# Attention into experts: the first item's last x slots turned by VectorE at the end of attention instead of by TensorE inside the expert stage

## The chip, the cores and the metric

One core of one Trainium2 chip. The time is the device time of one execution in microseconds (us), median of three runs. Engines are named as in the profile: PE is TensorE (PEld its weight loads), DVE is VectorE, ACT is ScalarE, POOL is GpSimd, SP is the engine that issues nearly all DMAs.

## What is computed

Attention with random features, whose output is the input of a mixture of experts with one expert per token:

```python
# attention: q, k, v are (4, 8, 576, 64), omega (128, 64)
q_p, k_p = phi(q * scale), phi(k * scale)   # phi(x): exp(h - max(h)) / sqrt(128), h = x @ omega.T - |x|^2 / 2
kv = einsum('bhsm,bhsd->bhmd', k_p, v)
num, den = einsum('bhsm,bhmd->bhsd', q_p, kv), einsum('bhsm,bhm->bhs', q_p, k_p.sum(2)) + 1e-06
x = (num / den).transpose(0, 2, 1, 3).reshape(2304, 512)
# experts: 8, capacity 576 each; w1 (8, 512, 1024), w2 (8, 1024, 512)
expert = argmax(x @ w_gate, 1); gate = softmax at expert
out[i] = gate[i] * (relu(x[i] @ w1[expert]) @ w2[expert])   # for tokens within the capacity, else 0
```

## The kernel before, in words

**Attention.** The main loop runs over steps: 18 for the keys, then t = 0 to 20 for the 18 tiles of 128 queries. Step t projects tile t on TensorE (pjq), transposes tile t - 2 (qtr), and accumulates numerator, denominator and gate logits of tile t - 3 into qacc (`numer`, L634). ScalarE exponentiates the two qtr banks into qpT (L802). `normalise` (L644) on VectorE divides: den (L650), rec (L652), xr (L653), and lg, the sum of the gate logits over the heads (L659). xr is written to x_d in HBM (L660). qacc has a single buffer, two PSUM banks, so the accumulation of the next tile starts when xr of the last one has been read.

**Experts.** An item is up to 576 slots of one expert. Its two matrix products use three float32r passes each: both operands are split into an upper part (hi, rounded) and a lower part (lo, the remainder). `mm1` (L666) makes one hi group: 12 matmuls for 128 rows of the hidden layer, over slots 0 to 255 (half 0) or 256 to 575 (half 1), followed by hhii (ScalarE, upper part after relu, L682) and hlo (VectorE, lower part, L685); hi groups go round three PSUM banks. x is needed with its 512 columns on the partitions: xhi and xlo are 128 x 4 x 576.

**The first item** is started inside attention. Its expert is known from the first token in step 3. Its x is the first 576 rows of attention's output. Tiles 0 and 1 (slots 0 to 255) are transposed on TensorE straight from xr in steps 5 to 8 (`FIRST_AT`). In step 15 `first_rows` (L625) loads x_d rows 256 to 639 with one DMA. Steps 18 to 20, when there is nothing left to project, each take one hi group of half 0 (`AHEAD`). After the loop the first item's other groups follow; ahead of the first three of these `transpose_x` (L394) transposes slots 256 to 575 on TensorE, 128, 128 and 64 at a time, and `copy_x` copies them to xhi (ScalarE, L408) and xlo (VectorE, L410).

**Later items** get x in another way. `load_x` (L380) loads 576 rows with four DMAs, one for each quarter of the columns, in blocks of 32 rows, and `turn_x` (L386) lets VectorE transpose 32 x 32 squares (L388). A column 4p + k then lies on partition p, part k, so w1 is loaded by rows 4p + k, `"(p k)"`, instead of rows 128k + p, `"(k p)"`, which the TensorE way needs. `run` and `start` work small tasks off between the parts of a step; the order of instructions on each engine is the order in which the program writes them.

```python
if 0 <= t - 3 < NT:                      # L814, end of a step
    normalise(t - 3, acc_l[0])
...
if j == 0 and k < 3:                     # L933, first item, ahead of a hi group
    for _ in transpose_x(2 + k, nm, (SM, 3, None)[k]):
        pass
mm1(f, half, hhi, hlo, hf, nm)()
```

Of the kernel before, what the change touches and what calls it, by code (L numbers as in the profile page):

```python
# [22 lines left out]
NT = N // 128  # L23
# [33 lines left out]
def attention_moe(ctx, tc, kT, qT, va, om, wg, w1, w2, cap, ident, tri, desc, lst, tab0, out):  # L57
# [83 lines left out]
    def start(gen):  # L141
        tasks.append([gen, None])

    def run(at=None, times=1, most=99):
        for _ in range(times):
            for task in list(tasks):
                if task[1] is None or (task[1] == at and most > 0):
                    most -= task[1] is not None
                    try:
                        task[1] = next(task[0])  # L150
                    except StopIteration:
                        tasks.remove(task)
# [197 lines left out]

    def load_w(i, c, ev, chunks_of="(k p)"):
        if i == 1:
            src = w1[ds(ev, 1), :, c * 256 : (c + 1) * 256].rearrange(f"o {chunks_of} f -> p (o k) f", p=128)
        else:
            src = w2[ds(ev, 1), c * 256 : (c + 1) * 256, :].rearrange("o (k p) f -> p (o k) f", p=128)
        nc.sync.dma_start(w_raw[i][c], src)
# [18 lines left out]
                in_offset=bass.IndirectOffsetOnAxis(ap=big["idx"][0:n, i, 2:3], axis=0),  # L377
            )

    def load_x(row):  # L380
        src = x_d[ds(row, SLOTS), :].rearrange("(b r) (q c) -> q r b c", r=32, q=4)
        for q in range(4):
            nc.sync.dma_start(big["xz"][32 * q : 32 * q + 32, :, :], src[q])


    def turn_x(b0, b1):  # L386
        t = big["xt"][:, 0 : b1 - b0, :].rearrange("p b (k r) -> p b k r", k=4)
        nc.vector.transpose(t, big["xz"][:, b0:b1, :].rearrange("p b (a k) -> p b k a", k=4))  # L388
        t = t.rearrange("p b k r -> p k b r")
        hi, lo = (big[x][:, :, 32 * b0 : 32 * b1].rearrange("p k (b r) -> p k b r", r=32) for x in ("xhi", "xlo"))  # L390
        nc.scalar.copy(hi, t)
        nc.vector.tensor_tensor(lo, t, hi.bitcast(F32), op=ALU.subtract)

    def transpose_x(i, nm, at):  # L394
        n = sub_n[i]
        tr = pair(f"xtr{nm}{i}") if at is None else bank(at, f"xtr{nm}{i}")
        for k in range(4):
            nc.tensor.transpose(
                tr[:, k * n : (k + 1) * n], big["xg"][0:n, i, k * 128 : (k + 1) * 128], id_sb[0:n, 0:n]
            )  # L400
        yield from copy_x(tr, i * SUB, n)
# [221 lines left out]
    xr_l = {}  # L623

    def first_rows():  # L625
        nc.sync.dma_start(
            big["xg"][:, 2:, :], x_d[2 * SUB : NSUB * SUB, :].rearrange("(i p) d -> p i d", p=SUB)
        )

    def numer(t, qpT, acc):  # L630
        for p in range(NP):
# [11 lines left out]

    def normalise(t, acc):  # L644
        xr = small.tile([128, ROW, H], F32, tag="xr", name=f"xr{t}", bufs=4)
        if t < 2:
            xr_l[t] = xr
        av = acc.rearrange("p (i x) -> p i x", i=2)[:, :, 0 : NP * ROW].rearrange("p i (h c) -> p c i h", c=ROW)
        den = small.tile([128, H], F32, tag="den", name=f"den{t}")
        nc.vector.tensor_scalar(den.rearrange("p (i h) -> p i h", i=2), av[:, D, :, :], EPS, None, op0=ALU.add)  # L650
        rec = small.tile([128, H], F32, tag="rec", name=f"rec{t}")
        nc.vector.reciprocal(rec, den)  # L652
        nc.vector.tensor_tensor(  # L653
            xr.rearrange("p c (i h) -> p c i h", i=2),
            av,
            rec.rearrange("p (i h) -> p i h", i=2).unsqueeze(1).to_broadcast([128, ROW, 2, NP]),
            op=ALU.mult,
        )
        nc.vector.tensor_reduce(lg[:, t, :], xr[:, D + 1 : ROW, :], op=ALU.add, axis=AX.X)  # L659
        nc.sync.dma_start(x_d[t * 128 : (t + 1) * 128, :], xr[:, 0:D, :].rearrange("p c h -> p (c h)"))  # L660

    HALVES = [(0, 256), (256, SLOTS)]

# [40 lines left out]
    for n in range(NK + NT + 3):  # L704
# [20 lines left out]
        if 0 <= t - 2 < NT:  # L725
            d = d_l.pop(t - 2)
            trs = [bank(3 + i, f"qtr{n}{i}") for i in range(2)]

            parts = [
                [(trs[i][:, u * 64 : (u + 1) * 64], d[64 * i : 64 * i + 64, u, :], i) for u in range(H)] for i in range(2)  # L730
            ]

            if t in FIRST_AT:
                k0 = FIRST_AT.index(t)
                i = k0 % 2
                tr = bank(SM, f"xtri0{k0}")
                rows = slice(64 * i, 64 * i + 64)
                x0 = xr_l[k0 // 2][:, 0:D, :].rearrange("p c h -> p (c h)")
                parts[i][0:0] = [
                    (tr[:, k * 64 : (k + 1) * 64], x0[rows, k * 128 : (k + 1) * 128], i) for k in range(4)  # L740
                ]
                start(copy_x(tr, 64 * k0, 64))
            for x in chain(*zip_longest(*parts)):
                if x is not None:
                    rows = slice(64 * x[2], 64 * x[2] + 64)
                    nc.tensor.transpose(x[0], x[1], id_sb[rows, rows])  # L746
# [42 lines left out]
        else:  # L789
# [24 lines left out]
            if 0 <= t - 3 < NT:  # L814
                normalise(t - 3, acc_l[0])
                if t == 3:
                    start(first_item())
            run(times=3)
        if 0 <= t < NT and t - QB[c] == 2 and c + 2 < len(QB) - 1:
            load_q(c + 2)  # L820
# [78 lines left out]
    with ExitStack() as ifs:  # L899
        for j in range(B):  # L900
# [15 lines left out]
            def prefetch():  # L916
                nonlocal row
                if last:
                    return
                ev = nc.sync.value_load(resd[0:1, 0, j : j + 1], min_val=0, max_val=E - 1)  # L920
                row = nc.sync.value_load(resd[0:1, 1, j : j + 1], min_val=0, max_val=N - S)
                load_x(row)
                for c in range(4):
                    load_w(1, c, ev, "(p k)")
                yield
                for c in range(4):
                    load_w(2, c, ev)
                yield

            pre = prefetch()  # L930
            for k, (f, half) in enumerate(STEPS[j > 0]):

                if j == 0 and k < 3:  # L933
                    for _ in transpose_x(2 + k, nm, (SM, 3, None)[k]):
                        pass
                mm1(f, half, hhi, hlo, hf, nm)()
                if j == 0:

                    listing(5 if k > 2 else 1)
                if j > 0 and k == 0:  # L940
                    next(pre, 0)
                if j == 0 and k < 6:
                    zero_out(k)
                if half == 0:
                    continue
                for i, c in HI_AT[j > 0].get(f, ()):
                    split_w_hi(i, c)
                for i, c in LO_AT[j > 0].get(f, ()):
                    split_w_lo(i, c)
# [89 lines left out]
    with ExitStack() as ifs:  # L1039
# [3 lines left out]
        for j in range(J):  # L1043
# [3 lines left out]
            sv = nc.sync.value_load(res[0:1, 1, j : j + 1], min_val=0, max_val=(E - 1) * REG + N)  # L1047
            load_idx(sv)
            for c in range(4):
                load_w(1, c, ev)  # L1050
            for c in range(4):
                load_w(2, c, ev)
            gather()
# [71 lines left out]
```

## Time and profile before

| | |
|---|---|
| median of three runs | 266.79 us (266.37 to 266.9) |
| the profiled execution | 267.14 us, its span 265.4 us |
| mean granted TensorE clock | 0.997 |
| TensorE, VectorE, ScalarE, GpSimd busy | 97%, 63%, 57%, 14% of the span |
| TensorE's transposes of x in the first item (L398) | 12, of 128 rows (8) and of 64 rows (4) |
| hi matmuls of three items (L675, L676, L677) | 576, over 256 or 320 columns |
| end of attention, first item's products | steps 18 to 20 from 98 to 108 us, mm1 until 131, mm2 until 157 |

The span runs from the first to the last instruction of the profiled execution, and the execution's own time has 1.7 us around it. Times in rows are us from the span's start. A row of a timeline has start, length, engine, line, operation, output<-inputs, shape, count, and in brackets how long the engine sat idle before it and for what.

### The profile page before, as it was taken

Reading aid. Unit: us, or ns where it says so; the run is one execution under the profiler, and the core shown is the slowest. Engines: PE = TensorE matmul, PEld = TensorE weight load, DVE = VectorE, ACT = ScalarE, POOL = GpSimd, SP = SyncE. Lnnn points to the kernel's source line nnn. Section 1 sums busy time; section 2 is a strip of 40 time slices with the busy share of each in tenths; the row PEclk is TensorE's granted clock in tenths of the full one; section 3 lists DMA queues with packets and bytes.
Section 4 is the critical chain, followed back from the end, with each engine's and each line's share of the span. In section 5 each row is a group of like instructions: output and inputs, shape, how many; then the busy total and the mean of one; then the engine's idle time right before and its main releaser. Section 6 shows DMA issues by size and latency. Waiting matters only on the chain.

```text
span 265.4 us, 7585 instructions
## 1 busy us (share of the span) xinstructions
PE 256.9 (97%) x3070; PEld 229.2 (86%) x3070; DVE 166.2 (63%) x329; ACT 150.6 (57%) x377; POOL 36.6 (14%) x54
## 2 busy tenths in 40 slices
PE   7999999999999999999999999999999999999990
PEld 6999999999999999999868889996888999958880
DVE  3789888869998994755763854443337443533570
ACT  4688888899999993436412455442354445224251
POOL 2100000143369893000000000000000000000000
PEclk9999999999999999999999999999999999999998
DMA  6999770035866767792079949900831892037211
GB/s 171 380 389 335 274 272 2 5 121 165 289 229 221 259 237 264 231 390 94 2 143 293 378 153 203 317 6 6 266 120 56 158 313 74 0 86 252 80 46 53
DMA packets 34130, 48.66 MB, mean 183 GB/s; under 512 B 2274, under 2 KB 21986, under 8 KB 34082
## 3 DMA queue, kind: packets, MB, share of 16 engines
q1 hardware_dynamic: 33506, 47.18, 56.4%
q10 hardware_dynamic: 576, 0.85, 0.9%
q8 instruction: 28, 0.46, 0.7%
q14 instruction: 20, 0.16, 0.2%
HBM read 36.10 MB, written 11.93 MB: 181 GB/s over the span
## 4 chain that ended last, share of the span: by engine, by line
PE 92%; ACT 3%; DVE 2%; issue 1%
PE hi L675 10%; PE hi L676 10%; PE hi L677 10%; PE yi L849 8%; PE yi L850 8%; PE pjk L165 8%; PE yi L851 8%; PE qacc L634 8%; PE pjq L165 6%; PE kacc L236 4%; PE kp L236 4%; PE qtr L746 3%; PE yi2r L861 1%; PE yi1r L861 1%; PE yi0r L861 1%
## 5 line engine op out<-in xcount | busy, mean ns | idle before, releaser
L675 PE MATMUL hi<-xhi,w1hi 128*128 128x256 f32 (+1 forms) x192 | 57.2, 298 | 0.0
L676 PE MATMUL hi<-xhi,w1lo 128*128 128x256 f32 (+1 forms) x192 | 56.4, 294 | 0.0
L677 PE MATMUL hi<-xlo,w1hi 128*128 128x256 f32 (+1 forms) x192 | 56.3, 293 | 0.0
L685 DVE SCALAR_TENSOR_TENSOR hloi<-hi,hhii 128x256 fp32r<-128x256 f32 x48 | 20.2, 421 | 40.1 <-ACT hfi L684 24.5
L682 ACT ACTIVATE hhii<-hi 128x256 fp32r<-128x256 f32 x48 | 18.4, 385 | 40.9 <-PE hi L677 40.8
L849 PE MATMUL yi<-w2hi,hhii 128*128 128x512 f32 x96 | 37.7, 393 | 0.0
L850 PE MATMUL yi<-w2hi,hloi 128*128 128x512 f32 x96 | 37.4, 389 | 0.0
L851 PE MATMUL yi<-w2lo,hhii 128*128 128x512 f32 x96 | 37.4, 389 | 0.0
L675 PEld LDWEIGHTS hi<-xhi,w1hi 128*128 128x128 f32 x192 | 36.0, 188 | 0.6 <-DVE hloi L685 0.2
L676 PEld LDWEIGHTS hi<-xhi,w1lo 128*128 128x128 f32 x192 | 36.0, 188 | 0.1
L677 PEld LDWEIGHTS hi<-xlo,w1hi 128*128 128x128 f32 x192 | 36.0, 187 | 0.0
L182 DVE TENSOR_REDUCE mx<-pjk 128x4 f32<-128x512 f32 (+1 forms) x38 | 23.2, 653 | 5.6 <-PE pjk L165 5.6
L796 POOL TENSOR_TENSOR d<-d,mx 128x512 f32<-128x512 f32 x18 | 18.7, 1039 | 54.0 <-DVE mx L182 49.7
L165 PE MATMUL pjk<-om_s,kraw 64*128 64x128 f32 x288 | 24.6, 307 | 0.6 <-DVE ex L783 0.6
L777 ACT ACTIVATE ex<-pjk,mx 128x128 f32<-128x128 f32 x72 | 20.6, 368 | 7.7 <-DVE mx L182 7.6
L849 PEld LDWEIGHTS yi<-w2hi,hhii 128*128 128x128 f32 x96 | 18.0, 188 | 6.1 <-issue 2.4
L634 PE MATMUL qacc<-kv_sb,qpT 128*64 128x73 f32 x576 | 22.5, 230 | 0.2 <-DVE e L587 0.2
L165 PEld LDWEIGHTS pjk<-om_s,kraw 64*128 64x128 f32 x288 | 21.1, 211 | 1.6 <-PE pjk L165 0.8
L165 PE MATMUL pjq<-om_s,qraw 64*128 64x128 f32 x288 | 21.4, 284 | 0.1
L851 PEld LDWEIGHTS yi<-w2lo,hhii 128*128 128x128 f32 x96 | 18.0, 188 | 3.8
L634 PEld LDWEIGHTS qacc<-kv_sb,qpT 128*64 128x64 f32 x576 | 19.8, 136 | 1.6 <-PE qtr L746 0.3
L850 PEld LDWEIGHTS yi<-w2hi,hloi 128*128 128x128 f32 x96 | 18.0, 188 | 3.6
(141 smaller groups left out, 406.0 us busy)
## 6 DMA issues: line engine op xcount, KB each, us to landing
w1raw<-w SPq DMA_DIRECT2D x16, 512.0 KB, 8.1
w2raw<-w SPq DMA_DIRECT2D x16, 512.0 KB, 6.4
qraw<-qT SPq DMA_DIRECT2D x6, 768.0 KB, 6.2
x_d<-xr SPq DMA_DIRECT2D x18, 256.0 KB, 3.3
v<-va SPq DMA_DIRECT2D x7, 650.0 KB, 6.9
kraw<-kT SPq DMA_DIRECT2D x6, 576.0 KB, 6.9
xg<-x_d SPq DMA_DIRECT2D x12, 288.0 KB, 5.4
out<-zero_sb SPq DMA_DIRECT2D x4, 768.0 KB, 7.3
```

Of the source, the lines that this page charges most:

```text
L165: nc.tensor.matmul(banks[i][:, k * M : (k + 1) * M], parts[k][rows, :], om_s[rows, :], start=True, stop=True)
L182: nc.vector.tensor_reduce(mx[:, a : a + src.shape[1]], src, op=ALU.max, axis=AX.X, negate=True)
L236: nc.tensor.matmul(acc[f : f + 64, i * 2 * VW + o : i * 2 * VW + o + (z - a) * VW], ex[:, 4 * i + k, f : f + 64], v[:, i, a * VW : z * VW] ...
L634: nc.tensor.matmul(acc[r : r + 64, i * 512 + p * ROW : i * 512 + (p + 1) * ROW], qpT[:, r // 64, (4 * i + p) * 64 : (4 * i + p) * 64 + 64] ...
L675: nc.tensor.matmul(pt, whi_[:, k, fs], xhi[:, k, sl], start=(k == 0), stop=False)
L676: nc.tensor.matmul(pt, wlo_[:, k, fs], xhi[:, k, sl], start=False, stop=False)
L677: nc.tensor.matmul(pt, whi_[:, k, fs], xlo[:, k, sl], start=False, stop=(k == 3))
L685: nc.vector.scalar_tensor_tensor(hlo[:, f, sl], pt[:, 0:w], 0.0, hhi[:, f, sl].bitcast(F32), op0=ALU.max, op1=ALU.subtract)
L777: nc.scalar.activation(ex[:, o + k, :], q[0][:, k * M : (k + 1) * M], AF.Exp, bias=mx[:, o + k : o + k + 1], scale=1.0)
L849: nc.tensor.matmul(pt, hhi[:, f, sl], w2hi, start=(f == 0), stop=False)
L850: nc.tensor.matmul(pt, hlo[:, f, sl], w2hi, start=False, stop=False)
L851: nc.tensor.matmul(pt, hhi[:, f, sl], w2lo, start=False, stop=(f == 7))
```

## The change

- The load in step 15 becomes `load_x` of rows 256 to 575: four DMAs of 160 KB, blocks of 32 rows.
- At the end of steps 18 and 19, behind `normalise`, `turn_x` turns five blocks (160 slots) each: transpose on VectorE (640 elements per partition), upper part on ScalarE, lower part on GpSimd.
- The twelve transposes on TensorE with their copies are dropped from the first item.
- Tiles 0 and 1 are still transposed on TensorE, but in the column order 4p + k: GpSimd copies the normalised tile into the buffer xt in this order, and TensorE transposes from there.
- w1 of the first item is loaded by rows 4p + k like that of the later items.

```diff
-    def load_w(i, c, ev, chunks_of="(k p)"):
+    def load_w(i, c, ev, chunks_of="(p k)"):
...
-    def load_x(row):
-        src = x_d[ds(row, SLOTS), :].rearrange("(b r) (q c) -> q r b c", r=32, q=4)
+    def load_x(rows, b0=0):
+        src = x_d[rows, :].rearrange("(b r) (q c) -> q r b c", r=32, q=4)
         for q in range(4):
-            nc.sync.dma_start(big["xz"][32 * q : 32 * q + 32, :, :], src[q])
-
-
-    def turn_x(b0, b1):
-        t = big["xt"][:, 0 : b1 - b0, :].rearrange("p b (k r) -> p b k r", k=4)
+            nc.sync.dma_start(big["xz"][32 * q : 32 * q + 32, b0:, :], src[q])
+
+
+    def turn_x(b0, b1, o=0, eng=nc.vector):
+        t = big["xt"][:, o : o + b1 - b0, :].rearrange("p b (k r) -> p b k r", k=4)
         nc.vector.transpose(t, big["xz"][:, b0:b1, :].rearrange("p b (a k) -> p b k a", k=4))
         t = t.rearrange("p b k r -> p k b r")
         hi, lo = (big[x][:, :, 32 * b0 : 32 * b1].rearrange("p k (b r) -> p k b r", r=32) for x in ("xhi", "xlo"))
         nc.scalar.copy(hi, t)
-        nc.vector.tensor_tensor(lo, t, hi.bitcast(F32), op=ALU.subtract)
+        eng.tensor_tensor(lo, t, hi.bitcast(F32), op=ALU.subtract)
...
     def first_rows():
-        nc.sync.dma_start(
-            big["xg"][:, 2:, :], x_d[2 * SUB : NSUB * SUB, :].rearrange("(i p) d -> p i d", p=SUB)
-        )
+        load_x(slice(32 * NBA, SLOTS), NBA)
...
     def normalise(t, acc):
...
+        if t < 2:
+
+            xr_l[t] = big["xt"][:, 4 * t : 4 * t + 4, :]
+            nc.gpsimd.tensor_copy(xr_l[t], xr[:, 0:D, :].rearrange("p c h -> p (c h)").rearrange("p (m k) -> p k m", k=4))
...
-                    (tr[:, k * 64 : (k + 1) * 64], x0[rows, k * 128 : (k + 1) * 128], i) for k in range(4)
+                    (tr[:, k * 64 : (k + 1) * 64], x0[rows, k, :], i) for k in range(4)
...
                 normalise(t - 3, acc_l[0])
                 if t == 3:
                     start(first_item())
+            if t in (NT, NT + 1):
+
+                b0 = NBA + 5 * (t - NT)
+                turn_x(b0, b0 + 5, b0 - NBA, nc.gpsimd)
             run(times=3)
...
-                if j == 0 and k < 3:
-                    for _ in transpose_x(2 + k, nm, (SM, 3, None)[k]):
-                        pass
                 mm1(f, half, hhi, hlo, hf, nm)()
```

Three places show how instructions move. In the rows, a number behind a name tells buffers of one name apart, and the brackets name the engines or DMA queues waited for.

TensorE, end of the loop into the first item: qacc is the last tile's accumulation, xtri the transposed x, hi a hi group. Before:

```order
L634 MATMUL qacc_2291<-kv_sb_75,qpT_2264 64x73 [waits DVE_49,PE_49,Activation_49]
L634 MATMUL qacc_2291<-kv_sb_75,qpT_2264 64x73 [waits Activation_49]
L634 MATMUL qacc_2291<-kv_sb_75,qpT_2264 64x73 x14
L398 MATMUL xtri_2330<-id_sb,xg 128x128 [waits DMAHW4_49]
L398 MATMUL xtri_2330<-id_sb,xg 128x128 x3
L675 MATMUL hi_2337<-xhi,w1hi_1003 128x256
```

With the change:

```order
L632 MATMUL qacc_2302<-kv_sb_75,qpT_2272 64x73 [waits DVE_49,PE_49,Activation_49]
L632 MATMUL qacc_2302<-kv_sb_75,qpT_2272 64x73 [waits Activation_49]
L632 MATMUL qacc_2302<-kv_sb_75,qpT_2272 64x73 x14
L675 MATMUL hi_2341<-xhi,w1hi_1003 128x256
L676 MATMUL hi_2341<-xhi,w1lo_1007 128x256
```

The transposes are gone, here and ahead of the next two hi groups; the wait of qacc for VectorE and ScalarE is as it was.

VectorE, from the end of step 18 into step 19: xr and lg close tile 15, hloi belongs to step 19's hi group, the next den to lg are tile 16. Before:

```order
L653 TENSOR_TENSOR xr_2207<-qacc_2183,rec_2210 128x584 [waits DMAHW2_49,DVE_49]
L659 TENSOR_REDUCE lg<-xr_2207 128x8 [waits DVE_49]
L685 SCALAR_TENSOR_TENSOR hloi_2168<-hi_2234,hhii_2167 128x256 [waits Activation_49]
L650 TENSOR_SCALAR den_2270<-qacc_2247 128x8 [waits PE_49]
L652 RECIPROCAL rec_2272<-den_2270 128x8 [waits DVE_49]
L653 TENSOR_TENSOR xr_2269<-qacc_2247,rec_2272 128x584 [waits DMAHW3_49,DVE_49]
L659 TENSOR_REDUCE lg<-xr_2269 128x8 [waits DVE_49]
```

With the change:

```order
L649 TENSOR_TENSOR xr_2212<-qacc_2188,rec_2215 128x584 [waits DMAHW2_49,DVE_49]
L655 TENSOR_REDUCE lg<-xr_2212 128x8 [waits DVE_49]
L388 STREAM_TRANSPOSE xt<-xg 128x640 [waits DMAHW6_49,DMAHW7_49,DMAHW5_49,DMAHW4_49]
L685 SCALAR_TENSOR_TENSOR hloi_2173<-hi_2242,hhii_2172 128x256 [waits Activation_49]
L646 TENSOR_SCALAR den_2278<-qacc_2255 128x8 [waits PE_49]
L648 RECIPROCAL rec_2280<-den_2278 128x8 [waits DVE_49]
L649 TENSOR_TENSOR xr_2277<-qacc_2255,rec_2280 128x584 [waits DMAHW3_49,DVE_49]
L655 TENSOR_REDUCE lg<-xr_2277 128x8 [waits DVE_49]
L388 STREAM_TRANSPOSE xt<-xg 128x640
```

A transpose stands ahead of each of the next two hloi, the first one waiting for the four loads.

ScalarE, the same steps: hhii of step 18, the two exponentials qpT and hhii of step 19. Before:

```order
L682 ACTIVATE hhii_2167<-hi_2170 128x256 [waits PE_49]
L802 ACTIVATE qpT_2264<-qtr_2216 128x512 [waits PE_49,Activation_49]
L802 ACTIVATE qpT_2264<-qtr_2217 128x512 [waits PE_49]
L682 ACTIVATE hhii_2167<-hi_2234 128x256 [waits PE_49]
L682 ACTIVATE hhii_2167<-hi_2278 128x256 [waits PE_49]
```

With the change:

```order
L682 ACTIVATE hhii_2172<-hi_2175 128x256 [waits PE_49]
L391 CAST xhi<-xt 128x4x160 [waits DVE_49]
L802 ACTIVATE qpT_2272<-qtr_2224 128x512 [waits PE_49,Activation_49]
L802 ACTIVATE qpT_2272<-qtr_2225 128x512 [waits PE_49]
L682 ACTIVATE hhii_2172<-hi_2242 128x256 [waits PE_49]
L391 CAST xhi<-xt 128x4x160 [waits DVE_49]
L682 ACTIVATE hhii_2172<-hi_2289 128x256 [waits PE_49]
```

The copy of the turned slots stands between hhii of step 18 and the exponentials of step 19, and a second one ahead of hhii of step 20.

## Rows read from the trace of the kernel before

**Rows 1.** The page: TensorE's and the other engines' busy time, chain by engine.

```profile
PE 256.9 (97%) x3070; PEld 229.2 (86%) x3070; DVE 166.2 (63%) x329; ACT 150.6 (57%) x377; POOL 36.6 (14%) x54
...
PE 92%; ACT 3%; DVE 2%; issue 1%
```

**Rows 2.** Timeline of TensorE from step 20 into the first item.

```profile
104.98 0.38 PE L675 MATMUL hi<-xhi,w1hi 128*128 128x256 f32 x1
...
106.55 1.25 PE L634 MATMUL qacc<-kv_sb,qpT 128*64 128x73 f32 x32
107.72 0.66 PE L398 MATMUL xtri<-id_sb,xg 128*128 128x128 f32 x4
...
113.49 0.31 PE L675 MATMUL hi<-xhi,w1hi 128*128 128x320 f32 x1
```

**Rows 3.** Timeline of TensorE, first two hi groups of the second item.

```profile
156.55 0.28 PE L675 MATMUL hi<-xhi,w1hi 128*128 128x256 f32 x1
...
157.96 0.31 PE L675 MATMUL hi<-xhi,w1hi 128*128 128x320 f32 x1
```

**Rows 4.** Timeline of VectorE, steps 18 to 20.

```profile
102.91 0.22 DVE L659 TENSOR_REDUCE lg<-xr 128x8 f32<-128x64 f32 x1
104.33 0.42 DVE L685 SCALAR_TENSOR_TENSOR hloi<-hi,hhii 128x256 fp32r<-128x256 f32 x1 [1.21 <-ACT hhii L682]
105.10 0.17 DVE L650 TENSOR_SCALAR den<-qacc 128x8 f32<-128x8 f32 x1 [0.35 <-PE qacc L634]
...
105.54 0.77 DVE L653 TENSOR_TENSOR xr<-qacc,rec 128x584 f32<-128x584 f32 x1
...
109.08 0.22 DVE L659 TENSOR_REDUCE lg<-xr 128x8 f32<-128x64 f32 x1
109.22 0.68 DVE L410 TENSOR_TENSOR xlo<-xtri,xhi 128x512 fp32r<-128x512 f32 x1
```

**Rows 5.** Timeline of ScalarE, step 19.

```profile
102.36 1.09 ACT L802 ACTIVATE qpT<-qtr 128x512 f32<-128x512 f32 x2 [1.49 <-PE qtr L746]
103.92 0.38 ACT L682 ACTIVATE hhii<-hi 128x256 fp32r<-128x256 f32 x1 [0.47 <-PE hi L677]
```

**Rows 6.** Groups by form, `turn_x` of later items: busy us, mean ns, idle before.

```profile
L388 DVE STREAM_TRANSPOSE xt<-xg 128x1280 f32<-128x1280 f32 x3 | 7.3, 2435 | 0.0
L388 DVE STREAM_TRANSPOSE xt<-xg 128x1024 f32<-128x1024 f32 x3 | 6.0, 1993 | 5.6 <-DMA xg<-x_d 5.6
...
L391 ACT CAST xhi<-xt 128x1280 fp32r<-128x1280 f32 x3 | 3.8, 1268 | 10.9 <-DVE xt L388 10.9
...
L391 ACT CAST xhi<-xt 128x1024 fp32r<-128x1024 f32 x3 | 3.1, 1042 | 3.8 <-DVE xt L388 3.8
```

**Rows 7.** Timeline of VectorE and ScalarE, first `turn_x` of the second item.

```profile
142.87 1.99 DVE L388 STREAM_TRANSPOSE xt<-xg 128x1024 f32<-128x1024 f32 x1 [5.63 <-DMA xg<-x_d]
...
144.89 1.05 ACT L391 CAST xhi<-xt 128x1024 fp32r<-128x1024 f32 x1 [3.78 <-DVE xt L388]
145.84 1.05 ACT L130 CAST w1hi<-w1raw 128x1024 fp32r<-128x1024 f32 x1
```

**Rows 8.** DMA issues: the page (KB each, us to landing) and SP's timeline.

```profile
xg<-x_d SPq DMA_DIRECT2D x12, 288.0 KB, 5.4
...
xg<-x_d SPq DMA_DIRECT2D x1, 768.0 KB, 4.7
...
94.15 0.43 SPq L626 DMA_DIRECT2D xg<-x_d  x1
...
133.65 2.01 SPq L383 DMA_DIRECT2D xg<-x_d  x4
```

**Rows 9.** Groups by form, GpSimd's two-input work.

```profile
L796 POOL TENSOR_TENSOR d<-d,mx 128x512 f32<-128x512 f32 x18 | 18.7, 1039 | 54.0 <-DVE mx L182 49.7 <-DVE den L650 2.2 <-DVE e L593 1.9
L133 POOL TENSOR_TENSOR w1lo<-w1raw,w1hi 128x256 fp32r<-128x256 f32 x16 | 11.4, 733 | 0.2
```

**Rows 10.** Timeline: tile 0 normalised, and its first transpose on TensorE.

```profile
58.33 0.77 DVE L653 TENSOR_TENSOR xr<-qacc,rec 128x584 f32<-128x584 f32 x1
...
61.77 0.22 PE L746 MATMUL xtri<-id_sb,xr 64*128 64x64 f32 x1
```

More of the change, by code (lines that the diff above doesn't have):

```diff
@@ L645, in normalise @@
         xr = small.tile([128, ROW, H], F32, tag="xr", name=f"xr{t}", bufs=4)
-        if t < 2:
-            xr_l[t] = xr
         av = acc.rearrange("p (i x) -> p i x", i=2)[:, :, 0 : NP * ROW].rearrange("p i (h c) -> p c i h", c=ROW)
@@ L737, in attention_moe @@
                 rows = slice(64 * i, 64 * i + 64)
-                x0 = xr_l[k0 // 2][:, 0:D, :].rearrange("p c h -> p (c h)")
+                x0 = xr_l[k0 // 2]
                 parts[i][0:0] = [
-                    (tr[:, k * 64 : (k + 1) * 64], x0[rows, k * 128 : (k + 1) * 128], i) for k in range(4)
+                    (tr[:, k * 64 : (k + 1) * 64], x0[rows, k, :], i) for k in range(4)
                 ]
@@ L921, in prefetch @@
                 row = nc.sync.value_load(resd[0:1, 1, j : j + 1], min_val=0, max_val=N - S)
-                load_x(row)
+                load_x(ds(row, SLOTS))
                 for c in range(4):
-                    load_w(1, c, ev, "(p k)")
+                    load_w(1, c, ev)
                 yield
@@ L1049, in attention_moe @@
             for c in range(4):
-                load_w(1, c, ev)
+                load_w(1, c, ev, "(k p)")
             for c in range(4):
```

## The prediction

> **What bounds the kernel now.** I read the page first, then the timelines around the place of the change. The page's engine line and its chain that ended last [rows 1] show one engine that decides: TensorE (PE) is busy for 97% of the span and carries 92% of the chain. So an edit is worth what it takes from TensorE's own queue, minus what it makes TensorE wait. VectorE (DVE, 63%), ScalarE (ACT, 57%) and GpSimd (POOL, 14%) have room on average, but an average says nothing about a single handover.
>
> The timeline of TensorE at the seam between attention and experts [rows 2] shows what the change removes. After the last accumulation (qacc, 106.55 to 107.72) stands a group of four transposes of x (L398), and two more such groups follow between the next groups of twelve hi matmuls; at 113.49 the first matmul over slots 256 to 575 (320 columns) starts. From 107.72 to 113.49, 5.77 us, TensorE does three hi groups of 256 columns and twelve transposes, without a pause.
>
> The timelines of VectorE [rows 4] and ScalarE [rows 5] of the same stretch show the handover that matters. Steps are numbered by t. In step 19 ScalarE exponentiates two tiles (102.36), then makes the upper part hhii of a hi group (103.92); VectorE takes the lower part hlo (104.33) and only then normalises tile 16 (den 105.10, xr 105.54, ended 106.31). qacc has one buffer, so TensorE's next qacc (106.55) may start only when that xr has been read. It comes 0.24 us earlier: no wait now, but that is all the spare time there is.
>
> **The sum, part by part.**
>
> *Twelve transposes leave TensorE.* A hi group of 256 columns between two other hi groups takes 157.96 - 156.55 = 1.41 us [rows 3]. With a change of kind of work on both sides it takes 106.55 - 104.98 = 1.57 [rows 2], so one change costs 0.08. Afterwards the three groups stand behind one qacc: 1.49 + 1.41 + 1.41 = 4.31 us instead of 5.77. **Saved: 1.46 us.**
>
> *Two VectorE transposes enter steps 18 and 19.* The trace has this instruction with 1280 and 1024 elements per partition, 2.435 and 1.993 us [rows 6]: 0.442 us for 256 elements, so 640 elements take 1.993 - 1.5 x 0.442 = 1.33 us. In plain proportion it would be 1.22; I take the line, since two sizes support it. The first is queued behind the sum lg of tile 15 (102.91). VectorE starts its next instruction about 0.08 us before the one ahead has ended (109.08 + 0.22 against 109.22 [rows 4]), so it starts at 103.05 and ends at 104.38.
>
> *ScalarE's copy (upper part) is what hurts.* It is queued in step 18, ahead of step 19's two exponentials and hhii, and needs the transposed tile. Its duration goes the same way: 1.268 and 1.042 us [rows 6] give 0.70 for 640 elements (0.63 in proportion). ScalarE starts 0.03 us after VectorE's transpose has ended and its next instruction 0.10 before the copy's end [rows 7]. So: copy 104.41 to 105.11; exponentials from 105.01 instead of 102.36, 1.09 us for both [rows 5]; hhii at 106.00; hlo 0.41 later (103.92 to 104.33 [rows 4, 5]) at 106.41; den at 106.75; xr 0.44 later, 107.19 to 107.96. TensorE's qacc of tile 17, ready at 106.55, starts at about 107.99. **Added: a wait of 1.44 us.** With the proportional durations it is 1.26; with 0.15 more for handovers that I cannot see in the rows, 1.6.
>
> *The second transpose, copy and the delayed tile 17 find room.* They run at 108.10 to 109.43 (VectorE) and 109.46 to 110.16 (ScalarE). hhii of step 20 follows at 110.06 and its hlo is done at 110.9; the hi group that needs its bank starts at 109.16 + 1.49 + 1.41 = 112.06. Tile 17 is normalised until about 112.2, the next hlo ends at 112.6, and its bank is wanted at 113.47: 0.9 us to spare. Routing starts after it, but each of its steps is tied to a later hlo and is on time again from the fourth group on. Three upper copies and three lower parts that VectorE and ScalarE had in 108 to 113 are gone.
>
> *GpSimd's two lower parts.* Its subtraction takes 0.733 us for 256 elements [rows 9], so 1.8 us for 640 in proportion, and at most 2.9 if each of the four pieces of 160 cost as much as 256. The second starts at 110.19 and must be there when the third matmul over slots 256 to 575 wants it, at 113.76. Covered by 3.6 us of TensorE's work: nothing. Without that cover it would cost its whole length.
>
> *GpSimd's two copies of normalised tiles.* Tile 0 is normalised at 59.10 and transposed on TensorE from 61.77 [rows 10]. Two-input work on 512 elements takes GpSimd 1.04 us [rows 9]. A copy has one input, so 0.52 at the least; 0.733 for each 256 elements gives 1.47 at the most. It ends by 60.6, over 1 us before TensorE wants it, and GpSimd's own next piece, whose result is used two steps later, is hardly pushed: both ends cost nothing. Tile 1 has a step more.
>
> *The load of the last slots* becomes four loads of 160 KB in place of one of 768 KB, issued at 94.15 [rows 8]; they were wanted at 107.72 and now at 103.05. The old load took 4.7 us [rows 8]. The same four-part load for the later items, 4 x 288 KB, was issued from 133.65 and let VectorE start at 142.87 [rows 7, 8]: 9.2 us beside weight loads. At that rate 640 KB take 5.1 us and land at 99.3; if size did not help at all they land at 103.35, 0.3 late. I take the first, with 3.7 us to spare. The Trainium skill speaks against this edit: "DMA: Bandwidth & Descriptors", section Bandwidth, asks for large transfers (6.15 us for 1 MB, 0.95 us for 64 KB). By its figures, an estimate, 160 KB take some 1.45 us and four in turn 5.8, longer than the old load but still before 103.05, so the sum would be the same. The order of w1's rows changes no size and no count of pieces (1 KB each): nothing.
>
> **Sum:** -1.46 + 1.44 = -0.02 us. The profiled execution took 267.14 us, 0.35 above the median of the three runs, 266.79; its successor should take 267.1, and the median **266.8 us**. The removed work comes back as a wait 1.2 us ahead of it. About 0.2%, 0.5 us, is what a measurement of this kernel can tell from no change.
>
> **Rivals.**
>
> *The wait does not arise, or is short* (faster). If VectorE's and ScalarE's extra work fitted beside TensorE's, the 1.46 us would stay: 265.3 us; with half the wait, 266.1. For it: nothing waits there before, and each engine alone has gaps. Against it: the queues are strictly in order, and the spare time is 0.24 us where 1.65 are put in. The point from which it pays is a transpose plus copy of less than about 1.4 us instead of 2.03. Chance 0.15.
>
> *The four loads come late* (slower). VectorE then stands at its first transpose with hlo, normalising and, through qacc, TensorE behind it; each microsecond after 103.05 is a microsecond more. It shows in the measurement from a landing at about 103.6, and the slowest pace that the rows allow gives 103.35 (267.1 us). Beside the w2 loads in the same stretch a landing at 104.2 is thinkable: 1.15 late, 267.9 us. Chance 0.10.
>
> *GpSimd is late* (slower). If its copy of tile 0 or its second lower part took more than twice the upper bounds above, TensorE would wait for it; 1 us late means 267.8 us. The rows give no reason. Chance 0.05. A wait larger by more than 0.5 us than worked out, from handovers of the three engines that add up, has 0.08: 267.4 us.
>
> That the transposes stay on TensorE is excluded by the order of the changed program.
>
> **How the numbers follow.** The forecast has 0.62: its own range is 266.4 to 267.3, from the bounds of the wait (-0.2 to +0.15 us) and the spread of the runs. Faster by over 0.2%: 0.15, the first rival. Slower: 0.10 + 0.05 + 0.08 = 0.23. The range that should hold the time 8 times in 10 takes in the half-hidden wait and most of a late load: 266.0 to 267.8 us.
>
> **What would show it.** Right: in the changed profile TensorE has a pause of about 1.4 us ahead of the last qacc, put down to VectorE's xr (or, in the chain, steps through VectorE and ScalarE there); three hi groups in a row without L398, the group of 320 columns within 0.3 us of where it was, counted from the start of step 18's hi group; the two 640-element transposes at 1.3 us, each behind lg; ScalarE's exponentials of step 19 some 2.6 us later than before. Wrong: a first transpose that waits for a load; a wait of a hi matmul for GpSimd; no pause ahead of qacc; or a later stretch, items 1 and 2, that changes its length.

## The result, and the profile after

Timed in turns with the kernel before on the same chip, the changed kernel takes 268.24 us (median of 10 runs, 267.61 to 269.37) against 266.86 (10 runs, 266.37 to 267.65): a ratio of 1.0051, interval 1.0037 to 1.0066. It is **slower by 1.4 us**, outside the range of the prediction and on the other side of its bound of 0.2%. The profiled execution took 267.61 us, the shortest of the ten, with a span of 266.0 us (before: 265.4). Ratios here and below leave out an execution more than 1.5% above the fastest of its kernel (one each in e2 and e6 below).

The page of the changed kernel has TensorE 1.6 us less busy than before and GpSimd 5.4 us more [rows 1]:

```profile
PE 255.3 (96%) x3058; PEld 227.9 (86%) x3058; DVE 166.9 (63%) x328; ACT 150.2 (56%) x376; POOL 42.0 (16%) x58
...
PE 91%; ACT 3%; DVE 2%; issue 1%
```

So twelve matmuls went from TensorE, and yet the time grew. First the seam. TensorE's timeline of the changed kernel, to be held against [rows 2] (start and duration in us, and in brackets the idle time before and who ended it):

```profile
104.85 0.38 PE L675 MATMUL hi<-xhi,w1hi 128*128 128x256 f32 x1
...
108.03 1.25 PE L632 MATMUL qacc<-kv_sb,qpT 128*64 128x73 f32 x32 [1.55 <-DVE xr L649]
109.21 0.38 PE L675 MATMUL hi<-xhi,w1hi 128*128 128x256 f32 x1
...
113.55 0.31 PE L675 MATMUL hi<-xhi,w1hi 128*128 128x320 f32 x1
```

The pause is there, 1.55 us, put down to VectorE's xr. Behind it stand three hi groups without a transpose, 109.21 to 113.55, 4.34 us in place of 5.77: 1.43 saved. The group of 320 columns starts at 113.55, where it was at 113.49. VectorE's and ScalarE's timelines (against [rows 4, 5]) show the chain that makes the pause:

```profile
102.77 0.22 DVE L655 TENSOR_REDUCE lg<-xr 128x8 f32<-128x64 f32 x1
102.95 1.35 DVE L388 STREAM_TRANSPOSE xt<-xg 128x640 f32<-128x640 f32 x1
...
106.69 0.16 DVE L646 TENSOR_SCALAR den<-qacc 128x8 f32<-128x8 f32 x1
...
107.12 0.77 DVE L649 TENSOR_TENSOR xr<-qacc,rec 128x584 f32<-128x584 f32 x1
```

```profile
104.33 0.73 ACT L391 CAST xhi<-xt 128x640 fp32r<-128x640 f32 x1 [3.61 <-DVE xt L388]
104.97 1.08 ACT L802 ACTIVATE qpT<-qtr 128x512 f32<-128x512 f32 x2
105.93 0.38 ACT L682 ACTIVATE hhii<-hi 128x256 fp32r<-128x256 f32 x1
```

The transpose starts directly behind lg, with no wait for a load: the four loads, issued from 94.02, had landed by 100.9, some 7 us after the first issue, where the one load had taken 4.7 [rows 8]. So the seam did what was forecast, and it does not explain 1.4 us. Nor does what follows: TensorE's last matmul starts at 258.29, where it was at 258.52 before. **The loss is behind the last work of TensorE.** The view of the program's last line (the instructions with which each engine's program closes, where the engines wait for one another, by engine: count, shortest, median and longest ns, first and last start in us; PEldq is TensorE's own instruction queue, DVEq is VectorE's) for the kernel before:

```profile
L1121 PEldq DRAIN  x2: 8/8/8, 263.8 to 264.9; - x2
...
L1121 DVEq EVENT_SEMAPHORE  x2: 21/21/21, 264.7 to 265.3; - x2
L1121 PEldq EVENT_SEMAPHORE  x2: 51/51/51, 264.7 to 265.3; - x2
```

and for the changed one:

```profile
L1121 PEldq DRAIN  x2: 8/8/8, 263.3 to 264.7; - x2
...
L1121 DVEq EVENT_SEMAPHORE  x2: 21/21/21, 264.6 to 265.2; - x2
L1121 PEldq EVENT_SEMAPHORE  x2: 51/51/51, 264.6 to 265.9; - x2
```

Before, all engines start their last instruction together at 265.3. Now the others do so at 265.2 and TensorE at 265.9: its last instruction comes 0.7 us late, 1.2 us after its own drain at 264.7, with no work left and no event that the profile could name as its releaser. That is 0.7 us of the loss; what makes up the rest is taken up below.

### The profile page after: what moved, and what is told of

Read it like the earlier page. It is cut to its first block, busy times and chain, and to the rows that moved or that the text cites. A ratio compares the mean times of both kernels' runs of the same rounds, so it can differ in the third digit from the quotient of the medians.

```text
span 266.0 us, 7566 instructions
## 1 busy us (share of the span) xinstructions
PE 255.3 (96%) x3058; PEld 227.9 (86%) x3058; DVE 166.9 (63%) x328; ACT 150.2 (56%) x376; POOL 42.0 (16%) x58
## 4 chain that ended last, share of the span: by engine, by line
PE 91%; ACT 3%; DVE 2%; issue 1%
PE hi L675 10%; PE hi L676 9%; PE hi L677 9%; PE yi L853 8%; PE yi L854 8%; PE pjk L165 8%; PE yi L855 8%; PE qacc L632 8%; PE pjq L165 6%; PE kacc L236 4%; PE kp L236 4%; PE qtr L746 3%; PE yi2r L865 1%; PE yi1r L865 1%; PE yi0r L865 1%
## 5 line engine op out<-in xcount | busy, mean ns | idle before, releaser
L675 PE MATMUL hi<-xhi,w1hi 128*128 128x256 f32 (+1 forms) x192 | 56.9, 296 | 0.0
L675 PEld LDWEIGHTS hi<-xhi,w1hi 128*128 128x128 f32 x192 | 36.0, 188 | 0.4
```

The source lines that it names most:

```text
L675: nc.tensor.matmul(pt, whi_[:, k, fs], xhi[:, k, sl], start=(k == 0), stop=False)
```

## The experiments

Two explanations stood against each other after this reading: a slower clock of TensorE behind the new pause, and a delay at the end of TensorE's program that has to do with the length of that program and not with the seam. e1 to e7 were timed in rounds beside the kernel before; e8 to e12 are one execution each. Below, the "end" of a run is read from the view just shown: TensorE's first drain, its first and its last semaphore instruction, and VectorE's last.

**Is it repeatable?** Both kernels again, unchanged, e1 the changed one, e2 the one before.

> The changed kernel, unchanged, for a second trace and for span and clock of every execution. Its first profile took 267.61 us, the fastest of its ten, with TensorE done 0.24 us earlier than before, so the median of 268.24 needs something that this profile does not show. Theory A (clock): the pause ahead of the last qacc lets the granted clock fall in some executions, by up to some 1.5 us; executions above 268 us then have a lower mean clock than before's 0.997, and a trace of one shows a stretch at half clock behind 108 us. Theory B (end of the program): the last instructions come later, as in the first profile, where TensorE's last semaphore ended 0.76 us after the other engines'; the spread is then in the part behind the last output, with TensorE done by 258.9. Both expect 1.004 to 1.006 of before.

> The kernel before, unchanged, beside it: 266.4 to 267.7 us, ratio 1.000. Theory A: mean clock near 0.997 in all executions, no stretch at half clock until TensorE is done. Theory B: the part behind the last output some 0.5 to 1 us shorter than in the changed kernel, at the same clock.

Measured: e1 268.52 us (267.65 to 269.09, 12 runs), 1.0037 [1.0021, 1.0053]; e2 267.09 (12 runs), 0.9988 [0.9974, 1.0002]. The kernel before, run beside both and e3 and e4, had a median of 267.43 (29 runs). The loss is real, some 1.0 to 1.4 us by the two ratios. In e1's trace TensorE's last matmul starts at 258.40 and in e2's at 258.68, so again the work ends 0.3 us earlier, and the end is later by more. The view of e1's last line:

```profile
L1121 DVEq EVENT_SEMAPHORE  x2: 21/21/21, 265.2 to 265.8; - x2
L1121 PEldq EVENT_SEMAPHORE  x2: 51/51/51, 265.2 to 267.1; - x2
```

TensorE's last instruction is 1.3 us behind VectorE's. How late it is differs from run to run.

**Take the pause away (e3).** The changed kernel, with ScalarE's copy of the split slots and GpSimd's lower part put behind hhii of the next step, so that they stand behind the exponentials and no longer ahead of them:

```diff
+        if eng is nc.gpsimd:
+            split_l.append((hi, lo, t))
+            return
         nc.scalar.copy(hi, t)
...
                 take()
+                while split_l:
+                    hi, lo, x = split_l.pop()
+                    nc.scalar.copy(hi, x)
+                    nc.gpsimd.tensor_tensor(lo, x, hi.bitcast(F32), op=ALU.subtract)
```

> The changed kernel with ScalarE's copy and GpSimd's lower part moved from the end of a step behind the next step's hhii, so that the exponentials no longer stand behind VectorE's transpose. By the sum of the prediction the pause of 1.4 to 1.55 us ahead of qacc goes and the 1.46 us saved on TensorE stay. Theory A: 1.5 us below before, 265.3, since no pause is left to lower the clock: ratio to before 0.994 to 0.995. Theory B: 1.55 us below the changed kernel, 266.7, and about level with before: 0.999 to 1.000, because the later end stays.

Measured: 266.96 us (266.7 to 269.3, 12 runs), 0.9994 [0.9972, 1.0015]. TensorE's timeline has no pause ahead of the last qacc, and the group of 320 columns starts 1.4 us earlier than in the changed kernel:

```profile
106.66 1.25 PE L637 MATMUL qacc<-kv_sb,qpT 128*64 128x73 f32 x32
107.84 0.39 PE L680 MATMUL hi<-xhi,w1hi 128*128 128x256 f32 x1
...
112.19 0.31 PE L680 MATMUL hi<-xhi,w1hi 128*128 128x320 f32 x1
```

Without the pause the kernel should beat the one before by about 1.4 us, and it only equals it (the interval reaches from a gain of 0.75 us to a loss of 0.4). The end shows where that went:

```profile
L1130 DVEq EVENT_SEMAPHORE  x2: 21/21/21, 263.5 to 264.1; - x2
L1130 PEldq EVENT_SEMAPHORE  x2: 51/51/51, 263.5 to 265.1; - x2
```

TensorE's last instruction is still late, by 1.0 us. The pause is worth its 1.5 us and the late end comes on top of it, independent of it.

**The pause alone (e4).** The kernel before, with one transpose and one copy of 640 elements put into steps 18 and 19 and their results overwritten later:

```diff
+            if t in (NT, NT + 1):
+                b0 = NBA + 5 * (t - NT)
+                x = big["xt"][:, b0 - NBA : b0 - NBA + 5, :].rearrange("p b (k r) -> p b k r", k=4)
+                nc.vector.transpose(x, big["xz"][:, b0 : b0 + 5, :].rearrange("p b (a k) -> p b k a", k=4))
+                nc.scalar.copy(
+                    big["xhi"][:, :, 32 * b0 : 32 * b0 + 160].rearrange("p k (b r) -> p k b r", r=32),
+                    x.rearrange("p b k r -> p k b r"),
+                )
```

> The kernel before with only the two transposes on VectorE and the two copies on ScalarE put at the end of steps 18 and 19 (their results are overwritten by the copies from TensorE's transposes, which stay). It has the pause but not the gain, and TensorE's instructions as before. Sum alone: before + 1.5 us, 268.3, ratio 1.0055. Theory A: + 1.5 and what the clock costs, about 2.8 us in all, 269.6, ratio 1.010. Theory B: + 1.5 only, with the end as before: 1.0055.

Measured: 268.69 us (6 runs), 1.0057 [1.0037, 1.0076], about 1.5 us more than before. TensorE's timeline:

```profile
108.29 1.25 PE L634 MATMUL qacc<-kv_sb,qpT 128*64 128x73 f32 x32 [1.50 <-DVE xr L653]
109.47 0.66 PE L398 MATMUL xtri<-id_sb,xg 128*128 128x128 f32 x4
```

The pause is 1.50 us, the loss 1.5 us, and the end is on time (TensorE and VectorE both at 266.8). So the pause brings nothing behind it. The clock says the same in the changed kernel. Its table of stretches (start and end in us, length, busy time of each engine with its instructions, granted clock, DMA share, GB/s):

```profile
106.00:108.00 2.00, 0.48 (x5) 0.28 (x3) 1.55 (x5) 0.32 (x2) 0.70 (x1) 1.00 0.23 84
108.00:114.00 6.00, 5.97 (x72) 5.92 (x73) 4.21 (x11) 2.03 (x5) 1.56 (x1) 1.00 0.60 187
114.00:258.00 144.00, 144.00 (x849) 124.51 (x848) 74.25 (x125) 59.98 (x121) 0.00 (x0) 1.00 0.55 160
```

The granted clock is 1.00 in the pause, right behind it and through the rest of TensorE's work: the upper level, 2.4 GHz. It falls only when TensorE's last matmul is over, as in the kernel before (0.53 from 263.4 to its end at 265.4). In the changed one:

```profile
263.40:266.00 2.60, 0.00 (x0) 0.00 (x0) 0.00 (x0) 0.00 (x0) 0.00 (x0) 0.51 0.04 9
```

The executions of e1 do have a lower mean clock (median 0.9915, the kernel before 0.995), which the expectation had named as a sign of the clock. Their traces show the lower level only in the idle end, which is longer, so it is no cause. The explanation by the clock falls.

**Give the removed instructions back where they never run (e5).** The changed kernel has 24 instructions fewer in TensorE's program (a transpose is a weight load and a matmul), and two semaphore instructions that are counted further below. e5 adds twelve transposes to the branch for leftover tokens, which is not taken with these inputs; e8 does the same to the kernel before:

```diff
+            if j == 0:
+                spare = bank(SM, "spare")
+                for _ in range(12):
+                    nc.tensor.transpose(spare[:, 0:128], big["xg"][:, 0, 0:128], id_sb)
             for f in range(8):
```

> The changed kernel with twelve 128-column transposes added to TensorE's code in the branch for leftover tokens, which is not taken here: nothing more is executed, but TensorE's program is as long again as before. If the extra time is the place of the end of TensorE's program, TensorE's last semaphore ends within 0.1 us of the other engines' (0.8 to 1.3 us behind them in the changed kernel), and the time falls by about 1 us to the level of before, ratio 1.000 to 1.001, with the pause of 1.55 us still there. If it is the clock or anything that runs, nothing changes: 1.004.

Measured: 267.39 us (266.55 to 268.75, 12 runs) against 266.98 for the kernel before (29 runs, which e6 and e7 share), 1.0015 [0.9988, 1.0042]. The page counts 7566 executed instructions, as in the changed kernel: nothing that runs was added. TensorE's timeline still has the pause:

```profile
107.62 1.25 PE L632 MATMUL qacc<-kv_sb,qpT 128*64 128x73 f32 x32 [1.55 <-DVE xr L649]
```

The late end is gone:

```profile
L1125 DVEq EVENT_SEMAPHORE  x2: 21/21/21, 264.5 to 265.1; - x2
L1125 PEldq EVENT_SEMAPHORE  x2: 51/51/51, 264.5 to 265.1; - x2
```

Of the loss of 1.0037 and 1.0051, 0.0015 are left, which this measurement cannot tell from nothing.

> The kernel before with twelve transposes added in the branch that is not taken: TensorE's program longer than in any of the others. One look at where its last semaphore ends: within 0.1 us of the others if only the shorter program is in a bad place, 0.8 us or more behind them if any other length than that of before is. The clock theory expects no difference.

One execution, 268.1 us, span 266.3; the 29 runs of the kernel before have spans of 264.3 to 268.3. TensorE and VectorE end together at 266.3, so this longer program has no late end; one execution says no more of its time.

**Take as many from the kernel before (e6, and e9 as one more execution).** In the same branch, which is not taken, the kernel before loses twelve matmuls. That leaves out part of the product for leftover tokens, of which these inputs have none.

```diff
+            short = nm == "l0" and f in (6, 7) and n == 1
...
-            nc.tensor.matmul(pt, wlo_[:, k, fs], xhi[:, k, sl], start=False, stop=False)
-            nc.tensor.matmul(pt, whi_[:, k, fs], xlo[:, k, sl], start=False, stop=(k == 3))
+            if not short:
+                nc.tensor.matmul(pt, wlo_[:, k, fs], xhi[:, k, sl], start=False, stop=False)
+            if not short or (f == 6 and k != 0) or k == 3:
+                nc.tensor.matmul(pt, whi_[:, k, fs], xlo[:, k, sl], start=False, stop=(k == 3))
```

> The kernel before with twelve matmuls left out of the same branch that is not taken (leftover tokens, two hi groups of the first list): what is executed is the kernel before, TensorE's program is as long as in the changed kernel. End of the program: TensorE's last semaphore 0.8 to 1.3 us behind the others, ratio 1.003 to 1.005. Clock or anything that runs: 1.000.

Measured: 268.81 us (268.49 to 272.89, 13 runs), 1.0054 [1.0026, 1.0082]. What runs is what ran before, 7585 instructions, and the kernel is 1.4 us slower by the ratio (1.8 between the medians). Here all engines are held, since TensorE is late two instructions earlier, between its drain and the first semaphore that the others wait for:

```profile
L1124 PEldq DRAIN  x2: 8/8/8, 265.2 to 268.5; - x2
...
L1124 DVEq EVENT_SEMAPHORE  x2: 21/21/21, 266.0 to 268.7; - x2
L1124 PEldq EVENT_SEMAPHORE  x2: 51/51/51, 268.3 to 268.7; - x2
```

> The kernel before with twelve matmuls fewer in the branch that is not taken, once more, since the first profile of it was of an execution 1.7 us above its median. End of the program: TensorE alone passes one of its last two semaphores 0.8 us or more later than the other engines, at 1 to 2 us above before. If the first profile was chance, all engines end within 0.1 us and the time is that of before.

One execution, 268.87 us beside 267.81 for the kernel before: drain at 263.5, first semaphore at 266.7, the same 3.2 us as in e6.

**Deferred and padded (e7).** e3 with the twelve transposes of e5: the pause and the late end both taken away.

> The deferred copy with the same twelve transposes in the branch that is not taken. End of the program: both gains stay, 1.46 us on TensorE and no late end: 1.3 to 1.6 us below before, ratio 0.994 to 0.995. Clock or anything that runs: as the deferred copy without them, 0.999.

Measured: 265.71 us (264.84 to 268.71, 12 runs), 0.9953 [0.9922, 0.9983]. It is the version that **beats both kernels**, by 1.3 us against the one before: nearly the 1.46 us that leave TensorE.

```profile
L1134 DVEq EVENT_SEMAPHORE  x2: 21/21/21, 262.3 to 262.9; - x2
L1134 PEldq EVENT_SEMAPHORE  x2: 51/51/51, 262.3 to 262.9; - x2
```

**How many instructions decide?** The changed kernel with one transpose in the branch (two instructions more), with four (eight more), and with four matmuls fewer (eight less; this leaves out part of the product for leftover tokens, of which there are none). The first two are the edit of e5 with `range(1)` and `range(4)`; the third is:

```diff
-            nc.tensor.matmul(pt, wlo_[:, k, fs], xhi[:, k, sl], start=False, stop=False)
+            if nm != "l0" or f != 7 or n != 1:
+                nc.tensor.matmul(pt, wlo_[:, k, fs], xhi[:, k, sl], start=False, stop=False)
```

> The changed kernel with one transpose more in the branch that is not taken, a weight load and a matmul. If the late end hangs on the last few instructions of TensorE's program lying behind a boundary, two instructions may move the late one by one or two places among TensorE's last, and the late end stays at 0.8 us or more; if any other length cures it, all end within 0.1 us.

> The changed kernel with four transposes more there, eight instructions. A boundary that lies among the last two or three instructions has then moved to before the end block: all engines end within 0.1 us, or the wait shows ahead of an earlier one of TensorE's end instructions, where other engines may still cover it.

> The changed kernel with four matmuls fewer in the branch that is not taken. If the boundary lies just ahead of the last instruction, a program shorter by eight instructions ends before it: all engines end within 0.1 us and the time is about 267. If any shorter program is late, TensorE's last semaphore stays 0.8 us or more behind.

One execution each, beside 267.81 us for the kernel before: 268.62, 267.38 and 266.6. The ends of all profiles together, read from the view of the last line (us). TensorE's instructions are counted against the changed kernel: two for each matmul, which has a weight load, and two semaphore instructions that went with the transposes (TensorE has one at L398 and four at L675 before, none and three after). So e6 and e9 are two instructions longer than the changed kernel, and not as long as it, as e6 was meant to be. The last column is when the last packet of DMA queue q8, of the kind "instruction", had ended, read from the DMA packets of the traces; it is taken up below.

| kernel | TensorE's program | first drain | first semaphore | last semaphore | VectorE's last | last q8 packet ended |
|---|---|---|---|---|---|---|
| before, e2, e4 | +26 | 263.8, 264.0, 265.4 | 264.7, 264.9, 266.2 | 265.3, 265.5, 266.8 | the same | 265.2, 265.9, 267.0 |
| e8 before padded | +50 | 264.8 | 265.7 | 266.3 | 266.3 | 266.2 |
| **after** | 0 | 263.3 | 264.6 | **265.9** | 265.2 | 264.7 |
| **e1** after again | 0 | 264.0 | 265.2 | **267.1** | 265.8 | 265.6 |
| **e3** deferred | 0 | 262.3 | 263.5 | **265.1** | 264.1 | 264.0 |
| e5 after, twelve pads | +24 | 263.3 | 264.5 | 265.1 | 265.1 | 265.0 |
| e7 deferred, twelve pads | +24 | 261.1 | 262.3 | 262.9 | 262.9 | 262.6 |
| e11 after, four pads | +8 | 263.7 | 264.9 | 265.5 | 265.5 | 265.1 |
| **e10** after, one pad | +2 | 263.3 | **266.4** | 266.8 | 266.8 | 265.1 |
| e12 after, four fewer | -8 | 263.0 | 264.2 | 264.8 | 264.8 | 264.3 |
| **e6, e9** before shortened | +2 | 265.2, 263.5 | **268.3, 266.7** | 268.7, 267.0 | 268.7, 267.0 | 267.0, 265.2 |

The number decides where TensorE is late. At 0 it is the last semaphore; at +2, in e10 and in e6 and e9 alike, it is the first semaphore, two instructions earlier; at -8, +8 and more nothing is late. So one fixed place in TensorE's instruction stream, which moves through the closing instructions as the program changes its length, fits all fourteen traces.

## Why the prediction was wrong

**The sum at the seam was right.** Forecast: 1.46 us saved, a wait of 1.44. Measured: 1.43 and 1.55. Its parts came as worked out: the transpose of 640 elements 1.35 us (1.33), the copy 0.73 (0.70), the exponentials at 104.97 (105.01), xr at 107.12 (107.19); the changed trace runs 0.14 us earlier in this stretch, so the last two came about 0.1 us late, which is the excess of the wait. From step 18's hi group, 98.63 in place of 98.77, to the group of 320 columns it is 0.20 us longer than before, inside the 0.3 that were named. e4 prices the pause alone at 1.5 us, and e7 against the kernel before prices the rest at -1.3.

**What was put at nothing there was nothing.** The loads: the transpose starts behind lg, though they landed at 100.9 and not at 99.3, with 2.0 us to spare instead of 3.7. GpSimd's lower parts: 1.57 us each, no hi matmul waits for them. GpSimd's copies of tiles 0 and 1: 1.15 us, between the bounds 0.52 and 1.47, and the first transpose of tile 0 starts at 61.73 (before 61.77 [rows 10]). The views by form of GpSimd:

```profile
L392 POOL TENSOR_TENSOR xlo<-xt,xhi 128x640 fp32r<-128x640 f32 x2 | 3.1, 1566 | 7.0 <-ACT xhi L391 7.0
...
L660 POOL COPY xt<-xr 128x512 f32<-128x512 f32 x2 | 2.3, 1145 | 0.4 <-DVE xr L649 0.3
```

**The rivals.** The pause arose, so the fast rival fell; no load came late for its transpose; GpSimd was not late; the pause exceeded its forecast by 0.11 us and not by 0.5. None of the slow rivals is what made it slow.

**The step that failed first** is the one at "Twelve transposes leave TensorE": it priced the removal by the time that the instructions had taken, and the sum went on to "-1.46 + 1.44 = -0.02 us" and so to the time of before. That step assumes that what follows the last matmul keeps its length whatever the program's length. It does not: the tail from TensorE's last matmul (start) to the end of the span grew from 265.4 - 258.5 = 6.9 us to 266.0 - 258.3 = 7.7, and in e1 to 267.2 - 258.4 = 8.8. None of the rows that the prediction read shows the end of the program, and no rival stood behind it. It also said that a later stretch of another length would speak against it. There is one, but small and the other way: from yi0r to yi1r in the chain it is 50.96 us against 51.26, and the same 0.3 in e1 against e2. Nearly all of it is one wait of TensorE for VectorE, which the kernel before has and the changed one has not:

```profile
161.32 0.19 PEld L675 LDWEIGHTS hi<-xhi,w1hi 128*128 128x128 f32 x1 [0.24 <-DVE hloi L685]
```

**A second step, smaller,** is the one at "The load of the last slots": it put the four loads at nothing because they land in time. They are also three DMAs more, and these moved the end. The last output lands at 263.58 before and at 263.13 after, and SyncE (SP), which has waited for it, then goes through the rest of its closing list. Of the first part of the list (L1039) two instructions are left before, seven after:

```profile
L1039 SPq EVENT_SEMAPHORE  x2: 17/17/17, 263.6 to 263.7; - x2
```

```profile
L1039 SPq EVENT_SEMAPHORE  x7: 17/17/17, 263.1 to 263.5; - x7
```

The list asks for eight DMA semaphores in turn, and the landing's is the seventh of them before and the second with three DMAs more. From the landing to VectorE's first closing semaphore it is 1.13 us in all six traces of kernels with the one load and 1.46 in all eight with four: **0.33 us** on every execution, in e5 and e7 too. No run changes the number of DMAs alone.

**What is shown and what is not.** Shown: the late end comes and goes with the number of instructions in TensorE's program, even of instructions that never run (e5, e6, e10, e11, e12), and with it about 0.6 to 1.0 us of the loss of 1.0 to 1.4 (e5 against e1 and the first comparison); the pause has no part in it (e3, e4). The traces add up: in the changed kernel's two profiles TensorE is 0.76 and 1.29 us late and SyncE's list is 0.33 longer, less the 0.23 and 0.28 by which the last matmul starts earlier, together 0.86 and 1.34; the last output's time from issue to landing, 3.3 to 4.2 us over the fourteen traces, scatters on top. What is left in e5, 0.4 us with an interval from -0.3 to 1.1, has room for the 0.33.

That TensorE waits there for its next instructions to be fetched is read from the traces, not from an experiment on the fetch. In every kernel the end of the program stands behind a branch that skips the code for leftover tokens, and TensorE stands at it for 3.6 to 4.4 us; before and after:

```profile
L1039 PEldq COMPARE_BRANCH  x1: 4111/4111/4111, 259.4 to 259.4; - x1
```

```profile
L1039 PEldq COMPARE_BRANCH  x1: 3871/3871/3871, 259.1 to 259.1; - x1
```

This wait is in both kernels and makes no difference between them. The page lists q8 in both as follows (packets, MB, share of the DMA engines' span), which makes 16 KB for each packet:

```profile
q8 instruction: 28, 0.46, 0.7%
```

In all fourteen traces TensorE leaves that branch 1.31 to 1.38 us after the last q8 packet but one has ended. The last packet is on its way while the closing instructions run. In the six traces with a late end the late instruction starts 1.1 to 1.5 us after this packet has ended, a delay near that at the branch; in the eight others the program's last instruction comes 0.5 us after it at most, or before it. So the late instruction waits for a packet that the others do not need. The profile does not say whose instructions q8 carries; that they are TensorE's is inferred from these times.

The Trainium skill ("Runtime: NRT & Kernel Launch", section Instruction fetch mechanics) states that each engine's instructions are fetched ahead in blocks of 256, in order, that crossing into a block is mostly hidden, and that a taken branch to a place outside the loaded blocks makes the engine wait for a fetch. The runs agree with the last: TensorE stands 3.6 to 4.4 us at the branch that is skipped. With "mostly hidden" they agree in the kernels whose end is on time, and not in the changed one, where 0.7 to 1.3 us lie open so soon behind the branch.

## What to carry to other kernels

Read the end of the program in both traces, behind the last matmul and the last store: when every engine's last instructions start, and whether one comes alone. A DMA more or less can move the end too, by where in SyncE's closing list the last landing stands. If an edit removes instructions and the time moves by about a microsecond that no stage shows, change the length of the latest engine's program by a few instructions in code that is not taken and time it again before you judge the edit. And in queues that are strictly in order, work that has time (here the upper copy) belongs behind the link that an engine waits for, not ahead of it: that move was worth about 1.6 us (268.52 us with the pause, e1, and 266.96 without, e3; 267.39 and 265.71, e5 and e7).

## What the runs showed of the hardware

TensorE can stand at the end of its program with nothing left to wait for that the profile shows: 1.2 us from its second drain to its last semaphore in the changed kernel, where the kernel before needs 0.4, and 3.1 to 3.2 us from its first drain to its first semaphore in e6, e9 and e10, where all others need 0.8 to 1.3. At the skipped branch it stands 3.6 to 4.4 us in every trace, 1.31 to 1.38 of them after an instruction packet of 16 KB has ended. SyncE takes about 0.065 us for each instruction of its closing list. Twelve matmuls fewer in a branch that is not taken made a kernel 0.54% slower. A strided copy of 512 elements took GpSimd 1.15 us, and its subtraction of 640 elements 1.57 us, less than the 1.8 in proportion to 256 elements at 0.733 [rows 9].
